# Attention times values of a head pair in two blocks, chunks ordered by size, the packed rows' tokens in one matmul

## The chip, the core and the metric

One core of a Trainium2 chip runs the whole program in one launch. The metric is the device time in microseconds; the median of the runs counts. The core has a matrix engine (PE, with its weight loads shown apart as PEld), a vector engine (DVE), a scalar engine (ACT), a general engine (POOL) and a queue engine (SP) that issues transfers. Each engine takes its instructions in the order in which they stand in its queue and waits on semaphores of the others.

## What is computed

The reference is causal attention with a cumulative bias, for 8 batches of 8 heads, 576 tokens and 64 dimensions, followed by a mixture of 8 experts with one expert for each of the 4608 tokens.

```python
scores = scale * np.matmul(q, k.transpose(0, 1, 3, 2))
s_pos = np.maximum(s, 0.0)
cum = np.cumsum(s_pos, axis=-1)
bias = -(cum[:, :, :, None] - cum[:, :, None, :])
scores = np.where(causal, -1000000000.0, scores + np.minimum(bias, 0.0))
scores = scores - np.max(scores, axis=-1, keepdims=True)
attn = np.exp(scores)
attn = attn / (np.sum(attn, axis=-1, keepdims=True) + 1e-09)
x = np.matmul(attn, v)          # then (batch, token, head * dim)
...
logits = x @ w_gate + modality_bias[modality_id]
e_idx = np.argmax(logits, axis=1)
for e in range(E):
    h = np.maximum(x[mask] @ w1[e], 0.0)
    out[mask] = gate_w[mask, None] * (h @ w2[e])
```

## The kernel before

The program has two stages. Attention fills a little less than the first half of the span, the experts (class `Moe`) the rest; the routing of tokens (class `Route`) runs in the background of both. The change touches attention alone.

**Pairs and chunks.** Attention works on 32 pairs. A pair is one head of two batches, called a and b. Its 2 x 576 query rows are cut into nine chunks: chunks 0 to 3 are 128 rows each of a, 4 to 7 the same of b, and chunk 8 holds the last 64 rows of a and the last 64 of b, packed into 128 partitions. Because of the causal mask, chunk c (or 4 + c) needs only 128(c + 1) keys, so chunks 3 and 7 are the largest (512 keys), 0 and 4 the smallest (128 keys, computed as 256), and chunk 8 needs 576.

**One chunk.** `score` issues two matmuls into an `sp` tile of PSUM (L228 and L229; four times two of 288 columns for chunk 8, L242 and L243). DVE adds the mask and takes the row extreme (L231, L245), ACT takes the exponential and the row sum into `sums` (L251). Three steps of the loop later (`LAG`) `trans` transposes the chunk, 128 x 128 at a time, on PE into a `pt` tile (L261; chunk 8 in L270, four into one tile and one into another). There are two `pt` buffers. ACT copies the transposed chunk to the SBUF tile `PT` (L264); for chunk 8 DVE does it (L276, four copies: a and b of the first tile, a and b of the second). So a transposition has to wait until the `pt` tile of the one before last has been copied out.

**The end of a pair.** `tail` multiplies the transposed weights by V: twelve matmuls with 64 output rows, a and b beside each other (L299 into `om` for queries 128 to 575, L297 into `ox` for queries 0 to 127). ACT and DVE copy the result to `oT` (L305, L306, L309), DVE adds a small number to the row sums and inverts them (`rs`, L303 and L304). Then two groups of small matmuls (`pw_`, L203) turn `oT` back to tokens and multiply it by the gate's weights in the same pass: two of 144 columns for each half, and in the second half two more of 72 columns for the packed tokens, one for a and one for b. DVE scales the result into `x` (L321, L323). Both halves use the same single `ox` buffer.

**The next pair's inputs.** `prep` splits the next pair's queries and keys into a high and a low part: POOL rounds them (L178: `QH`, `KA`, `KB`) and subtracts (L196, L198), and DVE makes one subtraction, the low part of a's queries (`QL`, L192). `QH` and `KA` have two buffers each, so POOL's first step for pair n + 1 waits until the last scores of pair n - 1 have read them.

**What sets the order.** `run` walks over pairs and over the nine chunks in the order of `ORDER`, and at each step issues a score, a step of `prep`, a step of the tail and a transposition. A scheduler then orders each engine's queue from this program order and its own estimates; `issue_after` ties the tail's matmuls behind those recorded before, and everything after them behind the last one (`wall`).

Of the kernel before, what the change touches and what calls it, by code (L numbers as in the profile page):

```python
# [7 lines left out]
F32 = mybir.dt.float32  # L8
# [4 lines left out]
ALU = mybir.AluOpType  # L13
# [18 lines left out]
class Attn:  # L32
# [71 lines left out]
    def setup(self, wg):  # L104
        nc = self.nc
        wgv = wg.rearrange("(h d) e -> d h e", d=64)
        for ab in range(2):
            nc.sync.dma_start(self.pw[64 * ab:64 * ab + 64, :, XW * ab + 64:XW * ab + XW], wgv)

    def consts(self, t1):  # L110
        nc = self.nc
# [23 lines left out]
        for ab in range(2):  # L135
            rows = slice(64 * ab, 64 * ab + 64)
# [3 lines left out]
        for ab in range(2):  # L140
            rows = slice(64 * ab, 64 * ab + 64)
            idv = self.ident[rows, 64 * ab:64 * ab + 64]
            nc.scalar.copy(self.pw[rows, :, XW * ab:XW * ab + 64], idv.unsqueeze(1).broadcast_to([64, 8, 64]))

    def rows0(self):
        nc = self.nc
        for u in range(2):
            nc.sync.dma_start(self.QL[u].bitcast(F32)[64:74], self.oh[:10])
            for ab in range(2):
                nc.sync.dma_start(self.KB[u].bitcast(F32)[74:76, ab], self.m1[:2])  # L150
# [124 lines left out]
                        w = PT[ab][:kp, PTW - 64:].unsqueeze(1)  # L275
                    cp(w, pt[:kp, :P * nj].rearrange("p (j a q) -> p a j q", a=2, q=64)[:, ab])  # L276

    def tail(self, st):

        nc = self.nc  # L280
        V, PT, x, h = st["V"], st["PT"], st["x"], st["h"]
        for _ in range(TD):
            yield
        o0 = self.ps2.tile([P, 512], F32, name="ox")
        om = self.ps2.tile([P, 448], F32, name="om")
        oT = self.oT[st["pi"] % 2]

        pe, self.pe = self.pe, []
        for j in (0, 1, 2, 3, 4, -1):
            q0 = max(P * j, P)  # L290
            for ab in range(2):
                r = slice(64 * ab, 64 * ab + 64)
                with ExitStack() as after:
                    for i in pe:
                        after.enter_context(self.tc.issue_after(i))
                    if j < 0:
                        m = nc.tensor.matmul(o0[r, :P], V[:, ab, 0, :], PT[ab][:, :P], start=True, stop=True)  # L297
                    else:
                        m = nc.tensor.matmul(om[r, q0 - P:], V[:, ab, j, :], PT[ab][:, PTS * j + q0 if j < 4 else PTW - 64:PTS * j + KW if j < 4 else PTW], start=j == 0, stop=j == 4)  # L299
                pe = [m.ins]  # L300
        self.wall = m.ins
        rs = self.sm.tile([P, 9], F32, name="rs")
        nc.vector.tensor_tensor(rs, st["sums"], self.eps, ALU.add)  # L303
        nc.vector.reciprocal(rs, rs)  # L304
        nc.scalar.copy(oT[:, :P], o0[:, :P])  # L305
        nc.scalar.copy(oT[:, P:512], om[:, :384])  # L306
        for ab in range(2):
            r = slice(64 * ab, 64 * ab + 64)
            nc.vector.tensor_copy(oT[r, 512 + 64 * ab:576 + 64 * ab], om[r, 384:])  # L309
        yield  # L310
        for g in range(2):
            xo = self.ps2.tile([P, 512], F32, name="ox")
            for u in range(2):
                c = 2 * g + u
                self.pw_(xo[:, 2 * XW * u:2 * XW * u + 2 * XW], oT[:, P * c:P * c + P], self.pw[:, h, :], start=True, stop=True)
            if g == 1:
                for ab in range(2):
                    self.pw_(xo[:, 4 * XW:5 * XW], oT[:, 512:], self.pw[:, h, XW * ab:XW * ab + XW], start=ab == 0, stop=ab == 1)
            src = xo[:, :4 * XW].rearrange("p (t d) -> p t d", t=4)
            rv = rs[:, 4 * g:4 * g + 4].unsqueeze(2).broadcast_to([P, 4, XW])  # L320
            nc.vector.tensor_tensor(x[g][:, :, :, h], src.rearrange("p t (d r) -> p t d r", r=2), rv.rearrange("p t (d r) -> p t d r", r=2), ALU.mult)  # L321
            if g == 1:
                nc.vector.tensor_scalar(x[2][:, 0, :, h], xo[:, 4 * XW:5 * XW].rearrange("p (d r) -> p d r", r=2), rs[:, 8:9], None, ALU.mult)  # L323
            yield

    def run(self, npair, newx, done, setup):

        bg = []
        self.load(1)
        seq = [(pi, i) for pi in range(npair) for i in ORDER]  # L330
        sts = {}
        prev, prepg, n = None, None, len(seq)
        for k in range(n + LAG + 9):
            if k < n:
                pi, i = seq[k]
                if k % 9 == 0:
                    sts[pi] = self.start(pi, newx(pi // 8) if pi % 8 == 0 else sts[pi - 1]["x"])
                    prepg = self.prep(pi + 1) if pi + 1 < npair else None
# [8 lines left out]
                    self.load(pi + 2)  # L347
                if prepg is not None:
                    next(prepg, 0)
            nt = None  # L350
            if LAG <= k < n + LAG:
                p0, i0 = seq[k - LAG]
                if i0 == ORDER[-1]:
                    nt = sts[p0]
            if prev is not None:
                if next(prev, 0) == 0:
                    prev = None
                    if ps["pi"] % 8 == 7:
                        bg.append(done(ps["pi"] // 8, ps["x"]))
            if LAG <= k < n + LAG:  # L360
# [4 lines left out]
            if prev is None and k >= n + LAG:  # L365
                break
            if bg and next(bg[0], 0) == 0:
                bg.pop(0)
        assert prev is None
        return bg  # L370


# [628 lines left out]
```

## Time and profile before

| | us |
|---|---|
| median of 3 runs | 925.4 |
| lowest and highest run | 919.98 and 928.19 |
| the profiled execution: its own time | 927.42 |
| its span | 925.7 |
| first matmul of the experts begins | 452.2 |

The profiled execution is one run; its time is 2.0 us above the median. In the timeline rows the columns are start, length, engine, line, operation, output tile <- inputs, shape, count, and in brackets the idle time of the engine before the row and what ended it. A count behind an x merges equal neighbours. Matmuls overlap, so on PE the distance from one start to the next says what a matmul costs, not its length.

### The profile page before, as it was taken

The numbers are of one execution on the slowest core, as the hardware profiler recorded it, in microseconds if no ns is written. First come the engines' busy times: TensorE is split into PE (matmuls) and PEld (weight loads), VectorE is DVE, ScalarE is ACT, GpSimd is POOL, SyncE is SP. The second block draws the span as 40 slices with busy tenths as digits, with TensorE's granted clock in tenths as the row PEclk, the third lists the DMA queues.
The fourth block names the chain that finished last, engine by engine and source line by source line (L and its number), as shares of the span: only waits on it lengthen the run. The fifth ranks groups of instructions, "written<-read, shape, count | busy, mean of one in ns | idle before, by whom it ended". The sixth has DMA issues, their size and how long they took to land. (4 is left out here: it accounts for less than half of the span.)

```text
span 925.7 us, 16704 instructions
## 1 busy us (share of the span) xinstructions
PE 836.3 (90%) x5584; PEld 697.8 (75%) x5584; DVE 622.3 (67%) x1486; ACT 521.4 (56%) x1209; POOL 573.5 (62%) x478
## 2 busy tenths in 40 slices
PE   0799998899889998799879989999999999999994
PEld 0577777677767776567669889999999999999962
DVE  7477777577867788666656966656666656666681
ACT  3577776677667776577434434545544445444651
POOL 9677777877697777853175536555655556555770
PEclk9999999999999999899989999999999999999998
DMA  5654445544544445520849758666666666665940
GB/s 148 197 136 137 137 136 150 176 134 133 173 149 151 125 133 179 229 83 3 277 164 332 282 203 301 236 221 228 230 225 219 224 223 224 223 228 220 336 160 2
DMA packets 67562, 172.76 MB, mean 187 GB/s; under 512 B 12087, under 2 KB 12087, under 8 KB 67412
## 3 DMA queue, kind: packets, MB, share of 16 engines
q1 hardware_dynamic: 61620, 151.64, 48.5%
q0 software_dynamic: 5856, 20.06, 5.5%
q8 instruction: 44, 0.72, 0.3%
q14 instruction: 42, 0.34, 0.1%
HBM read 144.95 MB, written 26.80 MB: 186 GB/s over the span
## 5 line engine op out<-in xcount | busy, mean ns | idle before, releaser
L251 ACT ACTIVATE pe<-pe,mx 128x512 f32<-128x512 f32 (+3 forms) x256 | 144.1, 564 | 48.7 <-DVE mx L231 46.7
L261 PE MATMUL pt<-ident,pe 128*128 128x128 f32 x640 | 121.1, 290 | 24.7 <-ACT PT L264 17.0
L231 DVE CUSTOM_DVE_ANT_0 pe<-sp,mk 128x512 f32<-128x512 f32 (+3 forms) x256 | 117.2, 481 | 22.9 <-PE sp L229 14.7
L264 ACT COPY PT<-pt 128x512 f32<-128x512 f32 (+3 forms) x256 | 106.6, 419 | 45.2 <-PE pt L261 34.6
L815 ACT ACTIVATE hT<-hp 128x512 fp32r<-128x512 f32 x72 | 42.8, 595 | 157.4 <-PE hp L813 156.5
L799 POOL DMA_INDIRECT out<-ys,oi x36 | 36.9, 1025 | 136.3 <-DVE ys L798 50.5
L261 PEld LDWEIGHTS pt<-ident,pe 128*128 128x128 f32 x640 | 79.9, 147 | 54.7 <-ACT PT L264 34.1
L228 PE MATMUL sp<-KA,QH 128*128 128x256 f32 (+2 forms) x256 | 98.2, 390 | 20.1 <-DVE KA L196 16.0
L196 POOL TENSOR_TENSOR KA<-rawk,KA 64x576 fp32r<-64x576 f32 x63 | 97.4, 1566 | 4.8 <-issue 2.3
L299 PE MATMUL om<-PT,V 128*64 128x448 f32 (+3 forms) x640 | 93.5, 435 | 0.0
L229 PE MATMUL sp<-KB,QL 76*128 76x256 f32 (+2 forms) x256 | 84.7, 334 | 7.2 <-DMA QL<-oh 7.2
L813 PE MATMUL hp<-xT,wcb 128*128 128x256 f32 x648 | 90.2, 283 | 0.0
L178 POOL TENSOR_SCALAR QH<-rawq 128x576 fp32r<-128x576 f32 x62 | 41.7, 674 | 74.6 <-issue 62.3
L816 DVE SCALAR_TENSOR_TENSOR hT<-hp,hT 128x512 fp32r<-128x512 f32 x72 | 49.3, 685 | 56.7 <-ACT hT L815 56.7
L813 PEld LDWEIGHTS hp<-xT,wcb 128*128 128x128 f32 x648 | 83.7, 189 | 0.6
L813 PE MATMUL hp<-xT,wcc 128*128 128x256 f32 x528 | 76.9, 286 | 7.9 <-DVE hT L816 3.2
L299 PEld LDWEIGHTS om<-PT,V 128*64 128x64 f32 x640 | 45.1, 142 | 48.8 <-issue 39.3
L792 PE MATMUL y<-wcb,hT 128*128 128x512 f32 x336 | 81.1, 398 | 0.0
L813 PE MATMUL hp<-xT,wca 128*128 128x256 f32 x552 | 78.2, 284 | 0.4 <-ACT xT L778 0.3
L813 PEld LDWEIGHTS hp<-xT,wcc 128*128 128x128 f32 x528 | 70.2, 194 | 9.2 <-DVE hT L816 3.4
L792 PEld LDWEIGHTS y<-wcb,hT 128*128 128x128 f32 x336 | 62.8, 188 | 14.8
L813 PEld LDWEIGHTS hp<-xT,wca 128*128 128x128 f32 x552 | 71.8, 190 | 1.3 <-ACT xT L778 0.5
(269 smaller groups left out, 1948.8 us busy)
## 6 DMA issues: line engine op xcount, KB each, us to landing
wrbw<-in_w SPq DMA_DIRECT2D x104, 512.0 KB
wraw<-in_w SPq DMA_DIRECT2D x56, 512.0 KB
rawq<-in_qkv SPq DMA_DIRECT2D x32, 576.0 KB
rawk<-in_qkv SPq DMA_DIRECT2D x32, 576.0 KB
xg<-lists SPq DMA_DIRECT2D x18, 576.0 KB
V<-in_qkv SPq DMA_DIRECT2D x32, 320.0 KB
lists<-z SPq DMA_DIRECT2D x8, 576.0 KB
ekd<-ek SPq DMA_DIRECT2D x1, 1440.0 KB
```

Of the source, the lines that this page charges most:

```text
L196: i = (nc.vector if pi == 0 and a == 0 else nc.gpsimd).tensor_tensor(KA[up, a], rk[up, a], KAf[up, a], ALU.subtract)
L228: self.pe.append(nc.tensor.matmul(sp[:, :nn], QH[:, q0:q0 + P], KA[:, ab, :nn], start=True, stop=False).ins)
L229: self.pe.append(nc.tensor.matmul(sp[:, :nn], QL[:EXT, q0:q0 + P], KB[:EXT, ab, :nn], start=False, stop=True).ins)
L231: ins = nc.vector.tensor_tensor_reduce(out=t[:, :n], in0=sp[:, :n], in1=self.mk[:, 512 - n:512], scale=-0.125, scalar=3.0e38, op0=ALU.add, ...
L251: nc.scalar.activation(t[:, :n], t[:, :n], AF.Exp, bias=m, scale=-1.0, accum_out=st["sums"][:, o:o + 1])
L261: self.pe.append(nc.tensor.transpose(out=pt[:, P * j:P * j + P], in_=pe[:, P * j:P * j + P], identity=self.ident).ins)
L264: cp(w[:, :, v:v + P], pt[:, :P * (c + 1)].rearrange("p (j q) -> p j q", q=P))
L299: m = nc.tensor.matmul(om[r, q0 - P:], V[:, ab, j, :], PT[ab][:, PTS * j + q0 if j < 4 else PTW - 64:PTS * j + KW if j < 4 else PTW], star ...
L792: self.last[0] = nc.tensor.matmul(y[u], hT[:, a, f, P * u:P * u + P], W[4 + f // 2][:, c, 512 * (f % 2):512 * (f % 2) + 512], start=f == 0 ...
L813: nc.tensor.matmul(hp[:, u], W[k][:, a, f:f + P], xT[:, c, k], start=k == 0 and i == 0, stop=k == 3 and i == 2)
L815: nc.scalar.activation(hs, hp, AF.Relu)
L816: nc.vector.scalar_tensor_tensor(hT[:, 1, 2 * m:2 * m + 2], hp, 0.0, hs.bitcast(F32), ALU.max, ALU.subtract)
```

## The change

Four things are changed in attention, and one tile shares its memory with another to make room.

- `ORDER` goes from (3, 7, 2, 1, 8, 6, 5, 0, 4) to (3, 7, 2, 6, 8, 1, 5, 0, 4): chunk 6 changes places with chunk 1, so that all chunks of the last queries come first.
- `tail` becomes two shorter tails for each pair. The first (`g` = 1), started when chunk 8 has been transposed, takes queries 256 to 575 in ten matmuls; the second (`g` = 0), started when the last chunk has been transposed, takes queries 0 to 255 in four. Each has its own `rs`, `oT` copy and `x`. The PSUM tiles `om` and `ox` become `o` (320 columns) and `ox`, one buffer each.
- In the first of these blocks the packed tokens come from one matmul of 72 columns with a new constant `pq` in place of two.
- `rs` is tied behind the latest row extreme (`hold`), the other matmuls' ties are looser within a step.

```diff
-ORDER = (3, 7, 2, 1, 8, 6, 5, 0, 4)
+ORDER = (3, 7, 2, 6, 8, 1, 5, 0, 4)
...
+        self.pq = c.tile([P, 8, XW], F32, name="pq")
...
-            s8 = t1.tile([64, KW], F32, name="s8")
+            s8 = sr
...
+            nc.sync.dma_start(self.pq[64 * ab:64 * ab + 64, :, 64:], wgv)
...
+            nc.scalar.copy(self.pq[rows, :, :64], idv.unsqueeze(1).broadcast_to([64, 8, 64]))
...
-    def tail(self, st):
+    def tail(self, st, g):
...
-        o0 = self.ps2.tile([P, 512], F32, name="ox")
-        om = self.ps2.tile([P, 448], F32, name="om")
+        q0, q1 = (256, KW) if g else (0, 256)
+        o = self.ps2.tile([P, 320], F32, name="o")
...
-        for j in (0, 1, 2, 3, 4, -1):
-            q0 = max(P * j, P)
+        nj = 5 if g else 2
+        for j in range(nj):
+            f = max(P * j, q0)
...
-                    if j < 0:
-                        m = nc.tensor.matmul(o0[r, :P], V[:, ab, 0, :], PT[ab][:, :P], start=True, stop=True)
-                    else:
-                        m = nc.tensor.matmul(om[r, q0 - P:], V[:, ab, j, :], PT[ab][:, PTS * j + q0 if j < 4 else PTW - 64:PTS * j + KW if j < 4 else PTW], start=j == 0, stop=j == 4)
-                pe = [m.ins]
+                    m = nc.tensor.matmul(o[r, f - q0:q1 - q0], V[:, ab, j, :], PT[ab][:, PTS * j + f if j < 4 else PTW - 64:PTS * j + q1 if j < 4 else PTW], start=j == 0, stop=j == nj - 1)
+            pe = [m.ins]
...
+        rs = self.sm.tile([P, 5], F32, name="rs")
+        with self.tc.issue_after(self.hold[0]):
+            nc.vector.tensor_tensor(rs[:, :n], st["sums"][:, 4 * g:4 * g + n], self.eps[:, :n], ALU.add)
+            nc.vector.reciprocal(rs[:, :n], rs[:, :n])
...
-            if g == 1:
-                for ab in range(2):
-                    self.pw_(xo[:, 4 * XW:5 * XW], oT[:, 512:], self.pw[:, h, XW * ab:XW * ab + XW], start=ab == 0, stop=ab == 1)
+        if g:
+            self.pw_(xo[:, 4 * XW:5 * XW], oT[:, 512:], self.pq[:, h, :], start=True, stop=True)
...
-            if nt is not None:
-                prev, ps = self.tail(nt), nt
+                if i0 in (8, ORDER[-1]):
+                    g = int(i0 == 8)
+                    prev.append((self.tail(sts[p0], g), sts[p0], g))
```

The lines below are instructions in the order in which they stand on an engine, in the middle of attention. Lines of the new program are three higher than those of the old around `score` and `trans` (L231 there is L228 before, L232 is L229, L264 is L261, L273 is L270, L279 is L276, L195 is L192, L267 is L264).

PE before, from the last two scores of a pair (256 columns, chunks 0 and 4) over the transposition of chunk 8 (`pep`) to the next pair's first scores (512 columns, chunks 3 and 7):

```order
L228 MATMUL sp<-KA_102,QH_98 128x256
L229 MATMUL sp<-KB_104,QL_100 128x256
L270 MATMUL pt<-ident,pep 128x128 x4
L228 MATMUL sp<-KA_102,QH_98 128x256
L270 MATMUL pt<-ident,pep 64x128
L229 MATMUL sp<-KB_104,QL_100 128x256
L228 MATMUL sp<-KA_103,QH_99 128x512
L229 MATMUL sp<-KB_105,QL_101 128x512
L228 MATMUL sp<-KA_103,QH_99 128x512
L229 MATMUL sp<-KB_105,QL_101 128x512
L261 MATMUL pt<-ident,pe 128x128 x5
```

The same place on PE now, from chunk 4's scores:

```order
L231 MATMUL sp<-KA_103,QH_99 128x256
L232 MATMUL sp<-KB_105,QL_101 128x256
L273 MATMUL pt<-ident,pep 128x128 x4
L273 MATMUL pt<-ident,pep 64x128
L231 MATMUL sp<-KA_102,QH_98 128x512
L232 MATMUL sp<-KB_104,QL_100 128x512
L264 MATMUL pt<-ident,pe 128x128 x2
L300 MATMUL o<-PT_108,V 64x320
L300 MATMUL o<-PT_106,V 64x320
```

Between chunk 8's transposition and the next one there is now one large score in place of two, and right behind that next transposition (chunk 1, two tiles) stands the first block of products with V.

DVE before, the stretch in which chunk 8's transposed tiles are copied out (L276), with the row extremes of the smallest chunks (`ISA`, 128 columns) around it:

```order
L321 TENSOR_TENSOR x<-ox,rs 128x144x2
L323 TENSOR_SCALAR xq<-ox,rs 128x36x2
L231 ISA pe,mx<-sp,mk 128x128
L231 ISA mx 128x1
L276 COPY PT_107<-pt 128x4x64
L276 COPY PT_108<-pt 128x4x64
L276 COPY PT_107<-pt 64x64
L276 COPY PT_108<-pt 64x64
L231 ISA pe,mx<-sp,mk 128x128
```

DVE now, the same stretch:

```order
L234 ISA pe,mx<-sp,mk 128x128
L234 ISA mx 128x1
L234 ISA pe,mx<-sp,mk 128x128
L234 ISA mx 128x1
L195 TENSOR_TENSOR QL_100<-rawq,QH_98 64x576
L279 COPY PT_108<-pt 128x4x64
L279 COPY PT_106<-pt 128x4x64
L279 COPY PT_108<-pt 64x64
L279 COPY PT_106<-pt 64x64
L234 ISA pe,mx<-sp,mk 128x512
```

The subtraction `QL` for the next pair now stands directly ahead of the copies in 24 of its 31 places; before, it stood behind the row extremes of the next pair's chunks 3, 7 and 2, and in none of them directly ahead of the copies.

ACT before, from the next pair's first exponential (512 columns) to the copy of chunk 3 (four tiles):

```order
L251 ACTIVATE pe,sums<-pe,mx 128x512
L264 COPY PT_108<-pt 128x2x128
L251 ACTIVATE pe,sums<-pe,mx 128x512
L264 COPY PT_107<-pt 128x128
L251 ACTIVATE pe,sums<-pe,mx 128x384
L264 COPY PT_108<-pt 128x128
L251 ACTIVATE pe,sums<-pe,mx 128x256
L264 COPY PT_106<-pt 128x4x128
```

ACT now:

```order
L254 ACTIVATE pe,sums<-pe,mx 128x512
L303 COPY oT_109<-o 128x256
L267 COPY PT_107<-pt 128x2x128
L267 COPY PT_106<-pt 128x128
L254 ACTIVATE pe,sums<-pe,mx 128x512
L267 COPY PT_107<-pt 128x128
L267 COPY PT_108<-pt 128x4x128
L254 ACTIVATE pe,sums<-pe,mx 128x384 x2
```

The copies of the small chunks no longer alternate one by one with exponentials of 512, 384 and 256 columns.

More of the change, by code (lines that the diff above doesn't have):

```diff
@@ new lines, in tail @@
+        rs = self.sm.tile([P, 5], F32, name="rs")
+        with self.tc.issue_after(self.hold[0]):
+            nc.vector.tensor_tensor(rs[:, :n], st["sums"][:, 4 * g:4 * g + n], self.eps[:, :n], ALU.add)
+            nc.vector.reciprocal(rs[:, :n], rs[:, :n])
+        xo = self.ps2.tile([P, 512], F32, name="ox")
+        for u in range(2):
+            c = 2 * g + u
+            self.pw_(xo[:, 2 * XW * u:2 * XW * u + 2 * XW], oT[:, P * c:P * c + P], self.pw[:, h, :], start=True, stop=True)
+        if g:
+            self.pw_(xo[:, 4 * XW:5 * XW], oT[:, 512:], self.pq[:, h, :], start=True, stop=True)
@@ L349, in run @@
                     next(prepg, 0)
-            nt = None
+            if prev and next(prev[0][0], 0) == 0:
+                _, st, g = prev.pop(0)
+                if g == 0 and st["pi"] % 8 == 7:
+                    bg.append(done(st["pi"] // 8, st["x"]))
             if LAG <= k < n + LAG:
                 p0, i0 = seq[k - LAG]
[L353 to L360, printed above, removed]
                 with self.behind():
                     self.trans(sts[p0], i0)
-            if nt is not None:
-                prev, ps = self.tail(nt), nt
-            if prev is None and k >= n + LAG:
+                if i0 in (8, ORDER[-1]):
+                    g = int(i0 == 8)
+                    prev.append((self.tail(sts[p0], g), sts[p0], g))
+            if not prev and k >= n + LAG:
                 break
@@ L368, in run @@
                 bg.pop(0)
-        assert prev is None
+        assert not prev
         return bg
```

32 lines of the change are left out of this document (12 added, 20 removed).

## The prediction

> **What bounds the kernel now.** I read first the busy time by windows, to see whether attention can be treated as one repeated pair. The columns are the window, its length, then busy time and count of PE, PEld, DVE, ACT and POOL, the granted clock, and the transfer engines' share and rate.
>
> ```profile
> 200.00:250.00 50.00, 46.15 (x337) 35.82 (x336) 38.39 (x142) 34.54 (x112) 34.67 (x37) 0.97 0.44 137
> 500.00:900.00 400.00, 394.27 (x2497) 353.73 (x2496) 268.41 (x293) 195.70 (x241) 233.73 (x105) 0.99 0.65 238
> ```
>
> In attention PE is busy 92% of the window and every other engine 77% or less. The experts keep PE busy 98%; the change doesn't touch their work, so what attention gains or loses reaches the end one to one.
>
> Next, the timeline of PE over one pair.
>
> ```profile
> 203.97 0.27 PE L261 MATMUL pt<-ident,pe 128*128 128x128 f32 x1
> 204.71 0.65 PE L261 MATMUL pt<-ident,pe 128*128 128x128 f32 x4 [0.46 <-ACT PT L264]
> 205.29 2.70 PE L299 MATMUL om<-PT,V 128*64 128x448 f32 x20
> ...
> 208.14 0.66 PE L261 MATMUL pt<-ident,pe 128*128 128x128 f32 x4
> ...
> 208.82 0.34 PE L229 MATMUL sp<-KB,QL 76*128 76x384 f32 x1
> 209.00 0.65 PE L203 MATMUL ox<-pw,oT 128*128 128x144 f32 x4
> 209.49 0.49 PE L261 MATMUL pt<-ident,pe 128*128 128x128 f32 x3
> ...
> 210.21 1.16 PE L203 MATMUL ox<-pw,oT 128*128 128x144 f32 x8
> 211.20 0.27 PE L261 MATMUL pt<-ident,pe 128*128 128x128 f32 x1
> 211.22 0.36 PE L228 MATMUL sp<-KA,QH 128*128 128x256 f32 x1
> 211.43 0.28 PE L229 MATMUL sp<-KB,QL 76*128 76x256 f32 x1
> 211.55 0.71 PE L270 MATMUL pt<-ident,pep 128*128 128x128 f32 x5
> 212.01 0.37 PE L228 MATMUL sp<-KA,QH 128*128 128x256 f32 x1
> ...
> 212.34 0.39 PE L228 MATMUL sp<-KA,QH 128*128 128x512 f32 x1
> ...
> 212.81 0.40 PE L228 MATMUL sp<-KA,QH 128*128 128x512 f32 x1
> ...
> 214.01 0.34 PE L229 MATMUL sp<-KB,QL 76*128 76x384 f32 x1
> 214.34 0.33 PE L261 MATMUL pt<-ident,pe 128*128 128x128 f32 x1
> ...
> 216.57 0.66 PE L261 MATMUL pt<-ident,pe 128*128 128x128 f32 x4 [0.46 <-ACT PT L264]
> ```
>
> From 204.71 to 216.57 a pair takes 11.86 us. PE is a nearly closed queue: five transpositions take 0.46 (211.55 to 212.01), about 0.1 each. What isn't work is a few waits. Between 203.97 and 204.71 one transposition takes 0.74, so about **0.63** is waiting: the four transpositions of chunk 3 need a `pt` tile that ACT hasn't emptied. From 214.01 to 214.34 the second half of a 384-column score takes 0.33 instead of 0.18 (208.82 to 209.00): **0.15**, again for `pt`. So the two `pt` buffers, and whoever empties them, are the weak place.
>
> **The change, part by part.** All terms are per pair.
>
> *The waits that go.* In ACT's new order chunk 0's copy precedes the 512-column exponential instead of following it, and chunks 4's and 3's stand together. A copy then waits for its transposition only, and 0.63 + 0.15 = 0.78 can go. If ACT still comes late, nothing goes. I take **-0.78**, bounds -0.78 and 0.
>
> *The packed tokens.* The group of four at 209.00 takes 0.49; the group of eight at 210.21, which has the two products of 72 columns besides, takes 0.99. The two cost at most 0.50, of which about 0.1 is the second group's wait for the single `ox`. One goes: **-0.20**, bounds -0.25 and -0.10. The wait for `ox` goes too, since other work now lies between the halves: **-0.10**, bounds -0.10 and 0.
>
> *The products with V in two blocks.* The columns summed over the matmuls of one half are 448 + 448 + 320 + 192 + 64 + 128 = 1600 before and 3 x 320 + 192 + 64 + 256 + 128 = 1600 now, so the streaming time stays. But a second block has its own borders. These are the weight loads at both borders of today's block:
>
> ```profile
> 205.29 0.20 PEld L299 LDWEIGHTS om<-PT,V 128*64 128x64 f32 x4 [0.17 <-issue]
> ...
> 208.14 0.42 PEld L261 LDWEIGHTS pt<-ident,pe 128*128 128x128 f32 x4 [0.17 <-PE om L299]
> ```
>
> The load starts only with its matmul, after 0.17 of idling, at each border: **+0.30** for two more borders, bounds +0.17 (one of the two hidden) and +0.40 (each with a little of the first matmul's start besides).
>
> *The new wait.* This is the term that decides. In the new PE order, chunk 8's transposition fills both `pt` tiles; one large score later stands chunk 1's transposition, which needs the first tile back, and the products with V are tied behind it. On DVE the copies that empty this tile now stand behind `QL`, which needs POOL's `QH`, which needs the last score of a to be done. Rows for this chain, first of the timeline, then of two views that group an operation's instructions (the first with shortest, median and longest in ns, the second with busy time and mean):
>
> ```profile
> 211.74 0.67 POOL L178 TENSOR_SCALAR QH<-rawq 128x576 fp32r<-128x576 f32 x1 [3.26 <-issue]
> 212.38 0.67 POOL L178 TENSOR_SCALAR KA<-rawk 128x576 fp32r<-128x576 f32 x1
> ...
> 203.17 1.17 DVE L192 TENSOR_TENSOR QL<-rawq,QH 64x576 fp32r<-64x576 f32 x1
> ...
> 204.40 0.25 ACT L264 COPY PT<-pt 128x128 f32<-128x128 f32 x1
> ...
> L192 DVE TENSOR_TENSOR QL<-rawq,QH x32: 741/1168/1495, 13.7 to 419.7; 64x576 fp32r<-64x576 f32 x32
> ...
> L276 DVE COPY PT<-pt 128x256 f32<-128x256 f32 x60 | 22.7, 419 | 5.8 <-PE sp L229 3.4 <-PE pt L270 1.7 <-PE sp L228 0.7
> ```
>
> I count from the start of chunk 0's score. PE's own work up to chunk 1's transposition is chunk 0, chunk 8's transposition, chunk 4 and one large score: the same four pieces that take 211.22 to 212.81 today, 1.59. The other path: POOL's `QH` starts 0.52 after (211.74), and POOL's next step begins at 212.38, so `QH` is done at 1.16, visible to DVE about 0.1 later (an estimate: ACT's copy ends at 204.65, PE goes on at 204.71). `QL` takes 1.17, two copies 0.42 each, 0.06 to PE: 1.16 + 0.10 + 1.17 + 0.84 + 0.06 = 3.33. PE waits 3.33 - 1.59 = **+1.74**. With the shortest `QL` in the row (0.74) it is +1.31; with the longest (1.50) +2.07.
>
> Which length of `QL` is right depends on POOL. The row at 203.17 ends at 204.34, and POOL's rounding before it ends at 203.74:
>
> ```profile
> 202.43 1.31 POOL L178 TENSOR_SCALAR KB<-rawk 64x576 fp32r<-64x576 f32 x2
> 203.82 3.18 POOL L196 TENSOR_TENSOR KA<-rawk,KA 64x576 fp32r<-64x576 f32 x2
> ```
>
> So `QL` ran 0.60 after POOL's instruction had ended, and seems to have stood still before. In the new place POOL goes from `QH` of a straight to its next 0.67 step before DVE hears of it; `QL` then stands about 0.57 and runs 0.60: 1.17 again, the value taken. The Trainium skill says the same in "SBUF — State Buffer", section "SBUF: two separate sides": the port pair that DVE and POOL share is an exclusive lock, held for a whole instruction, for a DVE operation with two SBUF inputs against a POOL operation that reads SBUF. By that rule the wait on PE is the +1.74, without it the +1.31; the trace agrees with the rule at 203.74.
>
> In 24 of 31 places `QL` stands directly ahead of the copies. In the other pairs the chain is chunk 8's transposition, two copies and chunk 1: the copies' 0.84 and about 0.2 for the matmul's end and hand-overs, less the large score of 0.47 (212.34 to 212.81): **+0.6**, bounds 0 and +0.9.
>
> *DVE's second `rs`.* One more addition and inversion of a few columns. The additions that stand today:
>
> ```profile
> L303 DVE TENSOR_TENSOR rs<-sums,eps x32: 155/652/3548, 39.4 to 442.9; 128x9 f32<-128x9 f32 x32
> ```
>
> The new one comes while POOL waits for the last score (the 3.26 of idling at 211.74), so I take 0.16 to 0.2, on DVE alone, and nothing on the path: its cover is that `QL` waits for POOL anyway. Without that cover it costs 0.5 more in each of the 24 pairs.
>
> *Routing.* Three times the counting matmuls of the router stand in PE's queue and wait for DVE:
>
> ```profile
> PE ox L501 <- DVE ohb L495: 7.4, 3, 2.5
> ```
>
> They move from inside the block of products to a place ahead of chunk 8's scores, with DVE busier. I take +1 each, **+3** in all, bounds -3 and +7.5 (the waits halve, or double). `pq` costs two transfers and two copies in the first pairs, hidden behind the 40 us before the first block; at worst 1 us. The transfers issued by SP in `prep` and `load` keep their loop steps, a pair ahead of use.
>
> **The sum.** For 24 pairs: -0.78 - 0.20 - 0.10 + 0.30 + 1.74 = +0.96, together +23.0. For the other 8: -0.78 - 0.20 - 0.10 + 0.30 + 0.6 = -0.18, together -1.4. Routing +3. In all **+24.6 us** on the profiled execution, 927.4 to 952. That execution lies 2.0 above the median of 925.4, so the median should be **950**.
>
> **Rivals.** About 1% (9 us) is what a measurement of this kernel can tell from no change.
>
> *Faster: the copies are not held.* If chunk 1's transposition finds its tile empty, the wait is 0 and each pair gains 0.78 + 0.20 + 0.10 - 0.30 = 0.78, 25 us in 32 pairs, 900. The point from which it decides is a new wait of 0.78. For it speaks that DVE idles a quarter of the window; against it, that DVE takes its queue in order, and even the shortest `QL` gives 1.31. Chance 0.07.
>
> *No change: a wait of about 0.8.* `QL` would need 0.74 and its start would have to come 0.5 earlier, with POOL not held by the last score; the 3.26 of idling at 211.74 speaks against it. 925. Chance 0.06.
>
> *Slower still: `rs` on the path.* If the first block's `rs` is held by a POOL instruction as today's is (0.65 in the middle of attention, 3.55 at most), it delays the row extremes of the small chunks and so `QL`: 0.5 in 24 pairs, 12 us more, 962. For it speaks the median of 652 in the row, against it POOL's idle time there. Chance 0.15.
>
> That the work is not what the change says is excluded by the order: ten and four products, one packed matmul.
>
> **Range and chances.** The forecast has 0.72. Its low end takes `QL` at 0.74 (-0.43 x 24 = -10) and routing at -3 instead of +3: 934. Its high end keeps half of ACT's waits (+0.39 x 32 = +12) and takes routing at +7.5 (+4.5): 966, which holds the third rival. With 2 us of spread below, that is 932 to 966, which leaves out the faster and the unchanged case, 0.13, and the tails. Slower by over 1%: 0.72 + 0.15 = 0.87; faster 0.07; the same 0.06.
>
> **What would show it.** Right: a PE row of two transpositions (chunk 1) with over 1.2 us of idling ahead, ended by DVE's `PT` copy, in 24 pairs; a pair of about 12.8 us; `QL` near 1.2 us and directly ahead of the copies in time; no 0.46 us of idling ahead of chunk 3's transpositions; two records of twelve fewer per pair in the small products of L203. Wrong: that idling missing or below 0.8, `QL` at 0.75, ACT rather than DVE ending PE's waits, or a pair below 11.9 us.

## The result and the profile after

| | before | after |
|---|---|---|
| time, median (lowest to highest), 4 runs each | 923.81 us (919.98 to 928.19) | 947.25 us (945.66 to 952.48) |
| ratio, with its 95% interval | | 1.0256 (1.023 to 1.0281): slower |
| the profiled execution: time, span | 927.42, 925.7 us | 945.66, 943.9 us |
| granted clock over the span | 0.974 | 0.977 |
| a plain pair, from the start of chunk 3's score to the next | 11.86 us | 12.62 us |
| start of the experts' first matmul (`hp`) in the span | 452.2 us | 469.0 us |
| from there to the end | 473.5 us | 474.9 us |

The profiles of e9 and e10 are of executions that ran slower than the others of the same kernel (1604.52 us and 971.14 us), so of these two kernels only the times are used.

The loss lies in attention: 16.8 of the 18.2 us between the two profiled executions have gone by when the experts begin. The same two windows as before, columns as there:

```profile
200.00:250.00 50.00, 44.84 (x348) 36.12 (x348) 35.58 (x139) 35.78 (x112) 33.68 (x36) 1.00 0.40 126
500.00:900.00 400.00, 393.63 (x2531) 357.09 (x2532) 260.40 (x292) 191.15 (x237) 224.69 (x103) 0.99 0.66 241
```

PE is busy 90% of the attention window instead of 92%. Over exactly one plain pair (200.48 to 212.34 before, 210.51 to 223.12 now), with a granted clock of 1.00 in both, its busy time falls from 11.40 to 11.18 us and its idle time grows from 0.46 to 1.43. The kernel isn't slower because PE has more to do; it waits more. The timeline of PE over the pair from the transpositions of chunk 3 and the short block of products to the second half of the small products (start, duration, and in brackets the idling ahead and what ended it):

```profile
204.92 0.60 PE L264 MATMUL pt<-ident,pe 128*128 128x128 f32 x4
...
206.53 0.87 PE L300 MATMUL o<-PT,V 128*64 128x256 f32 x8
207.34 0.65 PE L264 MATMUL pt<-ident,pe 128*128 128x128 f32 x4
...
208.07 0.66 PE L206 MATMUL ox<-pw,oT 128*128 128x144 f32 x4
208.56 0.49 PE L264 MATMUL pt<-ident,pe 128*128 128x128 f32 x3
...
209.42 0.36 PE L231 MATMUL sp<-KA,QH 128*128 128x256 f32 x1
...
210.82 0.40 PE L232 MATMUL sp<-KB,QL 76*128 76x512 f32 x1
212.66 0.41 PE L264 MATMUL pt<-ident,pe 128*128 128x128 f32 x2 [1.43 <-DVE PT L279]
212.99 2.27 PE L300 MATMUL o<-PT,V 128*64 128x320 f32 x20
215.20 0.44 PE L264 MATMUL pt<-ident,pe 128*128 128x128 f32 x2
...
215.94 0.65 PE L206 MATMUL ox<-pw,oT 128*128 128x144 f32 x4
216.43 0.34 PE L206 MATMUL ox<-pq,oT 128*128 128x72 f32 x2
216.61 0.27 PE L264 MATMUL pt<-ident,pe 128*128 128x128 f32 x1
```

Chunk 1's two transpositions at 212.66 stand still for 1.43 us, and DVE's copy of `PT` ends it. A score of 512 columns goes from its first half to the next instruction in 0.55 (the row at 215.39 to 215.94 in the same timeline), so the one that began at 210.51 would have let PE go on at 211.06. Counted from start to start the wait is therefore 1.60. DVE and POOL in the same stretch:

```profile
208.62 0.16 DVE L312 TENSOR_TENSOR rs<-sums,eps 128x4 f32<-128x4 f32 x1
...
209.94 1.30 POOL L181 TENSOR_SCALAR QH<-rawq 128x576 fp32r<-128x576 f32 x2 [3.92 <-issue]
...
210.64 1.20 DVE L195 TENSOR_TENSOR QL<-rawq,QH 64x576 fp32r<-64x576 f32 x1
...
211.77 1.00 DVE L279 COPY PT<-pt 128x256 f32<-128x256 f32 x4
...
216.85 0.31 DVE L312 TENSOR_TENSOR rs<-sums,eps 128x5 f32<-128x5 f32 x1
```

This is the predicted chain in time: `QH` starts 0.52 after chunk 0's score (209.42), `QL` takes 1.20 and ends at 211.84, the copies stand directly behind it, and PE goes on 3.24 us after that score. The waits of all engines over attention (in total, how often, the longest) show the same in sum, and a second thing. The first two rows are of the kernel before, from 50 to 452 us, the others of the changed kernel, from 50 to 469:

```profile
PE pt L261 <- ACT PT L264: 16.8, 31, 2.1
...
PE pt L261 <- DVE PT L276: 1.0, 2, 0.6
...
PE pt L264 <- DVE PT L279: 50.8, 31, 8.5
...
DVE QL L195 <- POOL QH L181: 15.5, 6, 6.7
...
PE pt L273 <- ACT PT L267: 3.9, 2, 3.8
```

PE's waits for ACT's copies are down from 16.8 us to 3.9 in two places. Those for DVE's copies grow from 1.0 to 50.8. In the timeline 19 of the 31 last 1.42 to 1.44 each; two last over 8 us. These two are where the router works in the background. The first of them:

```profile
168.43 0.96 POOL L523 DMA_INDIRECT lists<-xq,di  x1 [0.30 <-issue]
169.43 1.31 POOL L181 TENSOR_SCALAR QH<-rawq 128x576 fp32r<-128x576 f32 x2
170.14 1.21 DVE L195 TENSOR_TENSOR QL<-rawq,QH 64x576 fp32r<-64x576 f32 x1 [6.75 <-POOL QH L181]
...
172.16 0.66 PE L264 MATMUL pt<-ident,pe 128*128 128x128 f32 x2 [8.45 <-DVE PT L279]
```

POOL issues the router's transfers ahead of `QH`. `QL` stands idle 6.75 us for it on DVE, the copies behind `QL` wait with it, and PE waits 8.45. The three pairs there take 49.10 us instead of 44.02, the three of the second such place 47.82 instead of 43.84.

### The profile page after: what moved, and what is told of

It is laid out like the page before. It is cut to its first block, busy times and chain, and to the rows that moved or that the text cites. A ratio compares the mean times of both kernels' runs of the same rounds, so it can differ in the third digit from the quotient of the medians.

```text
span 943.9 us, 16901 instructions
## 1 busy us (share of the span) xinstructions
PE 823.7 (87%) x5648; PEld 697.1 (74%) x5648; DVE 634.6 (67%) x1550; ACT 522.4 (55%) x1211; POOL 577.0 (61%) x478
## 5 line engine op out<-in xcount | busy, mean ns | idle before, releaser
L264 PE MATMUL pt<-ident,pe 128*128 128x128 f32 x640 | 120.5, 287 | 51.1 <-DVE PT L279 50.8
L267 ACT COPY PT<-pt 128x512 f32<-128x512 f32 (+3 forms) x256 | 105.4, 422 | 87.8 <-PE pt L264 84.2
L234 DVE CUSTOM_DVE_ANT_0 pe<-sp,mk 128x512 f32<-128x512 f32 (+3 forms) x256 | 120.8, 485 | 30.3 <-PE sp L232 26.9
L264 PEld LDWEIGHTS pt<-ident,pe 128*128 128x128 f32 x640 | 76.2, 146 | 71.8 <-issue 60.9
L796 POOL DMA_INDIRECT out<-ys,oi x36 | 39.9, 1110 | 136.0 <-DMA out<-ys,oi 52.8
L231 PE MATMUL sp<-KA,QH 128*128 128x256 f32 (+2 forms) x256 | 100.7, 401 | 19.4 <-DVE KA L199 16.0
L300 PE MATMUL o<-PT,V 128*64 128x320 f32 (+4 forms) x896 | 105.6, 376 | 0.0
L300 PEld LDWEIGHTS o<-PT,V 128*64 128x64 f32 x896 | 60.7, 141 | 43.9 <-issue 15.4
L199 POOL TENSOR_TENSOR KA<-rawk,KA 64x576 fp32r<-64x576 f32 x63 | 89.6, 1441 | 4.6 <-DMA lists<-x,di 2.1
L232 PE MATMUL sp<-KB,QL 76*128 76x256 f32 (+2 forms) x256 | 83.3, 333 | 7.1 <-DMA QL<-oh 7.1
L813 DVE SCALAR_TENSOR_TENSOR hT<-hp,hT 128x512 fp32r<-128x512 f32 x72 | 49.2, 684 | 55.7 <-ACT hT L812 55.7
```

The source lines that it names most:

```text
L199: i = (nc.vector if pi == 0 and a == 0 else nc.gpsimd).tensor_tensor(KA[up, a], rk[up, a], KAf[up, a], ALU.subtract)
L231: self.pe.append(nc.tensor.matmul(sp[:, :nn], QH[:, q0:q0 + P], KA[:, ab, :nn], start=True, stop=False).ins)
L232: self.pe.append(nc.tensor.matmul(sp[:, :nn], QL[:EXT, q0:q0 + P], KB[:EXT, ab, :nn], start=False, stop=True).ins)
L234: ins = nc.vector.tensor_tensor_reduce(out=t[:, :n], in0=sp[:, :n], in1=self.mk[:, 512 - n:512], scale=-0.125, scalar=3.0e38, op0=ALU.add, ...
L264: self.pe.append(nc.tensor.transpose(out=pt[:, P * j:P * j + P], in_=pe[:, P * j:P * j + P], identity=self.ident).ins)
L267: cp(w[:, :, v:v + P], pt[:, :P * (c + 1)].rearrange("p (j q) -> p j q", q=P))
```

## The experiments

Every kernel ran beside the kernel before on the same chip. The median of the kernel before was 923.7 us beside e1 to e4, 923.8 beside e5 to e8, 931.2 beside e9 to e11 and 930.5 beside e12, so between these groups only ratios are compared. A pair is always a plain one, far from the router. Some of these kernels add a line or two, so line numbers differ by as much.

### e1: QL behind the copies

`QL` stays on DVE, but is tied behind the copies of chunk 8.

```diff
+                with self.tc.issue_after(self.t8) if self.t8 is not None else ExitStack():
                     nc.vector.tensor_tensor(QL[lo, a, :KW], rq[lo, a], QHf[lo, a, :KW], ALU.subtract)
...
-                    cp(w, pt[:kp, :P * nj].rearrange("p (j a q) -> p a j q", a=2, q=64)[:, ab])
+                    self.t8 = cp(w, pt[:kp, :P * nj].rearrange("p (j a q) -> p a j q", a=2, q=64)[:, ab]).ins
```

> The changed kernel with one thing different: on DVE the subtraction QL stands behind the four copies of chunk 8's transposed tiles instead of ahead of them; PE, ACT and POOL keep their order but for a few places around the router. Theory (PE waits at chunk 1's transposition because these copies are late): PE's wait there falls from 1.6 us to about 0.5, a plain pair from 12.62 to about 11.55 us, and the 8.5 us waits of the router's pairs go; in all 25 to 32 us less than the changed kernel, about 917 us, ratio to the kernel before 0.985 to 1.00. Rival 1 (two blocks of products cost their borders and more DVE steps): nothing of the loss depends on QL, 943 us or more, pair above 12.4. Rival 2 (QL is only moved, and delays the next pair's row extremes by as much): about half of the gain, 932 us.

Measured: 946.07 us, ratio 1.0211 (1.0143 to 1.0278), pair 12.47. The expectation missed: most of the wait went, the time did not. The timeline of one pair (PE, POOL, DVE, ACT in order of time):

```profile
209.17 0.41 PE L266 MATMUL pt<-ident,pe 128*128 128x128 f32 x2 [0.36 <-DVE PT L281]
...
211.95 2.80 POOL L201 TENSOR_TENSOR KA<-rawk,KA 64x576 fp32r<-64x576 f32 x2
...
213.37 1.40 DVE L314 TENSOR_TENSOR rs<-sums,eps 128x5 f32<-128x5 f32 x1
...
217.54 0.35 ACT L305 COPY oT<-o 128x256 f32<-128x256 f32 x1
217.94 0.76 PE L208 MATMUL ox<-pw,oT 128*128 128x144 f32 x4 [0.58 <-ACT oT L305]
```

Chunk 1's wait is 0.36 instead of 1.43. With it gone the long block of products ends earlier, its `rs` comes earlier on DVE, and now falls into the second of POOL's two subtractions (each 1.40): the addition of 5 columns, 0.31 in the changed kernel, takes 1.40. What stands behind it on DVE comes late, and PE now waits for `oT`. That it is `rs` was a guess here; e5 and e6 test it.

### e2: QL later still

```diff
+                with self.tc.issue_after(self.hold[0]) if self.hold[0] is not None else ExitStack():
                     nc.vector.tensor_tensor(QL[lo, a, :KW], rq[lo, a], QHf[lo, a, :KW], ALU.subtract)
```

> The changed kernel with QL tied behind the row extreme of the next pair's chunk 2 or 6, so far behind chunk 8's copies; the scheduler then puts the next pair's first row extreme (512 columns, 0.61 us) directly ahead of the copies, and the first large score ahead of chunk 8's transposition on PE. Theory (the copies' lateness after that transposition is what costs, whoever causes it): chunk 1's transposition follows chunk 8's directly, nothing on PE covers the copies, the wait stays near 1.4 to 1.7 us, pair about 12.6, 940 to 948 us. Rival (QL itself, held by POOL, is the cause): the wait goes with QL, pair 11.6, about 918 us.

Measured: 933.21 us, ratio 1.0105 (1.0068 to 1.0142), pair 12.20; between the two expectations. The tie moved more than `QL`:

```profile
199.77 0.74 DVE L196 TENSOR_TENSOR QL<-rawq,QH 64x576 fp32r<-64x576 f32 x1
...
204.40 1.04 PE L274 MATMUL pt<-ident,pep 128*128 128x128 f32 x5
...
204.71 0.69 DVE L235 CUSTOM_DVE_ANT_0 pe<-sp,mk 128x512 f32<-128x512 f32 x1 [0.17 <-PE sp L233]
...
205.13 0.11 PEld L274 LDWEIGHTS pt<-ident,pep 128*64 128x64 f32 x1 [0.38 <-ACT PT L268]
...
205.32 1.00 DVE L280 COPY PT<-pt 128x256 f32<-128x256 f32 x4
...
206.22 0.41 PE L265 MATMUL pt<-ident,pe 128*128 128x128 f32 x2 [0.78 <-DVE PT L280]
```

A row extreme of 512 columns now stands ahead of the copies where `QL` stood, and chunk 1's transposition idles 0.78 instead of 1.43. Counted from start to start the difference is smaller: PE takes 1.82 from chunk 8's first transposition (204.40) to chunk 1's (206.22), and these five transpositions take 0.52 in the changed kernel (209.99 to 210.51), so 1.30 is waiting instead of 1.60. A part of it lies ahead of chunk 8's fifth transposition, whose weights wait for a copy of ACT. The pair is 0.42 shorter, of which this wait makes 0.30. So it isn't `QL` as such: whatever DVE must do between PE's transposition of chunk 8 and the copies lies on the path. `QL` itself takes 0.74 here, where POOL's step ends 0.1 after it begins.

### e3: the order alone

The new `ORDER`; one block of products, `rs` and packed tokens as before.

```diff
-ORDER = (3, 7, 2, 1, 8, 6, 5, 0, 4)
+ORDER = (3, 7, 2, 6, 8, 1, 5, 0, 4)
```

> The kernel before with the new chunk order alone; one block of products with V, two packed matmuls. QL stands directly ahead of chunk 8's copies here too, in 20 pairs. Theory: chunk 8's copies are late again, but what waits for them on PE is not the products with V directly and more scores lie between; a pair 0.2 to 0.4 above 11.86, routing pairs longer by some us, 930 to 940 us. Rival (the loss comes from the split): equal to the kernel before, ratio 0.995 to 1.005.

Measured: 936.7 us, ratio 1.014 (1.0112 to 1.0168), pair 12.33. The time is as expected, the pair a little longer (0.47 above the kernel before, expected were 0.2 to 0.4). `QL` with its 1.20 stands ahead of the copies here too; PE waits 0.58 for them.

### e4: the split alone

The two blocks, the second `rs` and the packed matmul with the old order; the long block comes after chunk 6.

```diff
-ORDER = (3, 7, 2, 6, 8, 1, 5, 0, 4)
+ORDER = (3, 7, 2, 1, 8, 6, 5, 0, 4)
...
-                if i0 in (8, ORDER[-1]):
-                    g = int(i0 == 8)
+                if i0 in (6, ORDER[-1]):
+                    g = int(i0 == 6)
```

> The changed kernel with the old chunk order; the block for the last queries starts when chunk 6 has been transposed. QL stands directly ahead of chunk 8's copies in 3 pairs alone. Theory: without the late copies the split costs its two more borders (0.2 to 0.3) and saves the packed matmul and the wait for ox (0.3) and part of ACT's waits: a pair of 11.4 to 12.1 us, 915 to 938 us. Rival (two blocks are what costs): a pair of 12.4 or more, 943 us or more.

Measured: 955.59 us, ratio 1.0358 (1.0306 to 1.041), pair 12.46. The theory as it was written there missed; the time and the pair lie where the rival put them. DVE and PE in the timeline:

```profile
215.69 1.20 DVE L195 TENSOR_TENSOR QL<-rawq,QH 64x576 fp32r<-64x576 f32 x1
...
216.82 0.44 DVE L322 TENSOR_TENSOR x<-ox,rs 128x288 f32<-128x288 f32 x1
217.18 1.00 DVE L279 COPY PT<-pt 128x256 f32<-128x256 f32 x4
...
218.07 0.74 PE L264 MATMUL pt<-ident,pe 128*128 128x128 f32 x5 [0.64 <-DVE PT L279]
```

The split by itself puts `QL` and, behind it, the product of the small matmuls with `rs` (L322) ahead of the copies. So each half of the change brings about the same neighbourhood on DVE. The plain pair is 0.60 longer than before; most of the loss lies elsewhere. The four pairs around each of the router's first two places take 67.2 and 65.0 us, counted from chunk 8's score, instead of 55.9 and 55.7 in the kernel before: 20.6 of the 28.2 us by which the experts start later (480.5 instead of 452.2). The losses aren't additive: 1.4% for the order and 3.6% for the split with its packed matmul, and 2.56% for all of it.

### e5 and e6: rs without its addition, with and without e1's tie

In both, `rs` is the reciprocal of the sums; the addition of 1e-9 is left out. The reciprocal has one SBUF input, the addition two.

```diff
-            nc.vector.tensor_tensor(rs[:, :n], st["sums"][:, 4 * g:4 * g + n], self.eps[:, :n], ALU.add)
-            nc.vector.reciprocal(rs[:, :n], rs[:, :n])
+            nc.vector.reciprocal(rs[:, :n], st["sums"][:, 4 * g:4 * g + n])
```

e5 has e1's tie besides:

> The kernel of e1 (QL behind chunk 8's copies) and rs without its addition: the reciprocal is taken of the row sums themselves, so the addition of 1e-9 (a DVE operation on two SBUF tiles) is left out. Theory (in e1 the wait moved to the second block's rs, which stood 1.40 us behind POOL's subtraction KA; the next row extremes, exponentials and the oT copy of the first block were late by it): PE's 0.58 us wait for ACT's oT goes, only the 0.36 ahead of chunk 1's transposition stays, a plain pair falls from 12.47 to 11.5 to 11.8, the whole to 915 to 928 us, no slower than the kernel before by more than 0.5%. Rival (the two blocks' own work on PE, their borders, is what remains): pair 12.2 or more, 938 us or more.

Measured: 914.29 us, ratio 0.9897 (0.9873 to 0.9922), pair 11.37; a little better than expected, and about 1% faster than the kernel before. e6 has `QL` where the change puts it:

> The changed kernel with rs without its addition and nothing else changed (1e-9 left out as in e5). Theory: in the changed kernel rs takes 0.16 to 0.31 and chunk 1's wait for QL decides; a pair stays at 12.3 to 12.65, 938 to 947 us. Rival (rs is the cause by itself): 12.0 or less, below 930 us.

Measured: 942.64 us, ratio 1.0206 (1.0179 to 1.0232), pair 12.62, as expected. e5 and e6 differ by the place of `QL` alone, and that is worth 28 us and 1.25 in each plain pair. Each edit alone takes the ratio from 1.0256 to 1.0211 and to 1.0206, half a per cent that the intervals don't separate from nothing; the two together gain 3.6%. So there are two waits, one behind the other: `QL` ahead of the copies hides that `rs` would be held by POOL, and the gain of the first edit shows only when the second is made.

### e7 and e8: the same edits in the kernel before

e7 leaves the addition out of `rs` in the kernel before:

```diff
-        nc.vector.tensor_tensor(rs, st["sums"], self.eps, ALU.add)
-        nc.vector.reciprocal(rs, rs)
+        nc.vector.reciprocal(rs, st["sums"])
```

> Control: the kernel before with rs without its addition (1e-9 left out). There rs takes 0.65 us and stands between the two row extremes of chunk 8, ahead of ACT's largest exponential, which the products with V cover. Theory: DVE is not late there, a pair stays at 11.7 to 11.86, 918 to 924 us. Rival (any DVE time is worth its length): 0.65 in 32 pairs, 903 us.

Measured: 923.63 us, ratio 1.0004 (0.9988 to 1.002), pair 11.86. In the kernel before `rs` costs nothing, though its addition took 0.65 there; its cover held.

e8 makes the packed matmul alone, with the constant `pq` and its room as in the change:

```diff
...
-                for ab in range(2):
-                    self.pw_(xo[:, 4 * XW:5 * XW], oT[:, 512:], self.pw[:, h, XW * ab:XW * ab + XW], start=ab == 0, stop=ab == 1)
+                self.pw_(xo[:, 4 * XW:5 * XW], oT[:, 512:], self.pq[:, h, :], start=True, stop=True)
```

> The kernel before with the packed tokens in one matmul and nothing else. Theory: PE is the closed queue, a matmul less is worth its 0.20 to 0.25 us in each of 32 pairs, 6 to 8 us, 916 to 918 us, ratio 0.990 to 0.994. Rival (the time is taken back by the next wait for a pt tile): ratio 0.997 to 1.002.

Measured: 916.04 us, ratio 0.9909 (0.988 to 0.9937), pair 11.64. Of the change's three parts this one is a gain, 0.22 per pair.

### e9 and e12: a third pt tile

The changed kernel with three `pt` tiles, and three `sp` tiles instead of four to make room. It tests the other half of the wait: that PE needs a tile, not the data in it.

```diff
-SPB = 4
+SPB = 3
...
-            pt = self.ps1.tile([P, 512], F32, name="pt")
+            pt = self.ps1.tile([P, 512], F32, name="pt", bufs=3)
...
-                pt = self.ps1.tile([P, 512], F32, name="pt")
+                pt = self.ps1.tile([P, 512], F32, name="pt", bufs=3)
```

> The changed kernel with three pt tiles instead of two, paid for with three sp tiles instead of four. Theory (chunk 1's transposition waits for the tile that chunk 8's copies empty, and these stand behind QL): that transposition then takes the third tile, which was emptied before, and its 1.4 us of idling goes. But the copies themselves come no earlier, and the block of products behind needs them: PE waits there instead, for 1.60 less chunk 1's own 0.41, about 0.8 to 1.2, ended by DVE's copy of PT. Pair 11.9 to 12.3, 925 to 938. Rival (the tile isn't what it waits for, or one score tile less costs as much): pair 12.6 or more, 943 or more.

Measured: ratio 1.0006 (0.9985 to 1.0027). The whole loss is gone, a little more than expected. Where PE waits is read from e12, which is the same kernel:

> The kernel of e9_third_pt once more, for a profile of it in which TensorE's matmuls have their usual durations (in e9's they last about twice as long, so no wait shows). Its time was that of the kernel before, 1.0006 times. Theory: the ratio is within 0.995 to 1.005 again, the pair is 11.8 to 12.0, and what is left of the wait (0.7 to 1.2 per pair) stands ahead of the five-chunk block of products, ended by DVE's copy of PT, not ahead of chunk 1's transposition. Rival (the tile only hid part of the wait, and the rest came from elsewhere): chunk 1's transposition still waits over 0.5, or the pair is below 11.4 with the time lost outside the plain pairs.

Measured: ratio 1.0001 (0.9975 to 1.0026), pair 12.15. One pair, DVE and PE:

```profile
205.51 1.20 DVE L195 TENSOR_TENSOR QL<-rawq,QH 64x576 fp32r<-64x576 f32 x1 [0.40 <-POOL QH L181]
...
206.65 1.00 DVE L279 COPY PT<-pt 128x256 f32<-128x256 f32 x4
...
207.11 2.60 PE L300 MATMUL o<-PT,V 128*64 128x320 f32 x20 [0.85 <-DVE PT L279]
```

`QL` and the copies stand as in the changed kernel. Chunk 1's transposition no longer waits. The block of products does, for the copies' data: 0.85 instead of 1.43, and ended by the same operation. The pair is longer than the 11.8 to 12.0 expected, and 0.29 longer than before. The time is nevertheless that of the kernel before. From the first pair's score of chunk 3 to the last pair's this profile is 7.6 us longer than that of the kernel before (420.4 instead of 412.8); the last pair's way from there to the first `hp` gives back 5.0 (18.4 us, 436.4 to 454.8, instead of 23.4, 428.8 to 452.2). The other 2.6 can't be placed, since that profile of the kernel before was taken on another occasion, at 927.42, and the kernel before ran at 930.5 beside e12.

### e10: the copies on ACT

```diff
-PTDVE = (8,)
+PTDVE = ()
```

> The changed kernel with chunk 8's two copies on ACT instead of DVE; QL stays where it is. Theory (QL on DVE's queue holds the copies): the wait ahead of chunk 1's transposition falls from 1.4 to below 0.6 and is ended by ACT; pair 11.5 to 12.0, 912 to 928, with ACT 0.8 busier per pair. Rival (the copies would be late on any engine, behind ACT's exponentials): the wait stays over 1.0, pair 12.3 or more, 937 or more.

Measured: ratio 1.0098 (1.0064 to 1.0133), between the two expectations. Taking the copies off DVE's queue recovers 1.6 of the 2.56%. What holds up the rest is not shown.

### e11: e5 with a third pt tile

The edits of e5 and of e9 together.

> The kernel of e5_ql_and_rs (QL behind the copies; rs as the reciprocal of the sums alone, the addition of 1e-9 left out) with three pt tiles and three sp tiles. Theory (with QL behind, chunk 1 waits 0.24 for the copies and little else is left of pt): at most 0.24 in 24 pairs to gain, 6 us: 908 to 914. Rival (one score tile less holds up the scores behind the exponentials): 0.2 or more per pair lost, 920 or more.

Measured: 908.28 us (907.61 to 908.48), ratio 0.9755 (0.9734 to 0.9777), pair 10.93. In us it lies in the expected range, but that range was written for a kernel before of 923.8, and this chip's is 931.2: by the ratio it is better than expected, and the best version found. The pair is 0.44 shorter than e5's, not 0.24. The same place in e5,

```profile
207.44 0.40 PE L233 MATMUL sp<-KA,QH 128*128 128x512 f32 x1
...
208.31 0.41 PE L266 MATMUL pt<-ident,pe 128*128 128x128 f32 x2 [0.24 <-DVE PT L281]
208.65 2.27 PE L302 MATMUL o<-PT,V 128*64 128x320 f32 x20
```

and in e11:

```profile
214.75 0.39 PE L266 MATMUL pt<-ident,pe 128*128 128x128 f32 x2
214.89 0.48 PE L233 MATMUL sp<-KA,QH 128*128 128x512 f32 x1
...
215.54 2.28 PE L302 MATMUL o<-PT,V 128*64 128x320 f32 x20
```

The score and the two transpositions go from 207.44 to 208.65, 1.21, in e5, and from 214.75 to 215.54, 0.79, in e11. By this comparison the wait that the profile showed as 0.24 of idling cost 0.42 from start to start. e11 also leaves the addition of 1e-9 out, as e5 does; the reference has it.

## Why the prediction was right, point by point

The forecast was 950 (932 to 966), slower; the result is 947.25. On the profiled executions the sum was +24.6, and +18.2 was measured. That execution of the kernel before lay 3.6 above the median of its four runs, that of the changed kernel 1.6 below its own, so the medians differ by 23.4. That the median came out within 3 us of the forecast is therefore luck in part; the profiled sum was off by 6.4. By its steps:

- **ACT's waits go (-0.78).** Right in the place: where 0.46 of idling stood ahead of chunk 3's transpositions there is none (204.92), and of `pt` waits on ACT 3.9 us are left in all. The 0.78 itself was not measured singly.
- **Packed tokens and `ox` (-0.20 - 0.10).** Right. The two halves of the small products took 0.49 + 0.99 before and take 0.49 (208.07 to 208.56) + 0.67 (215.94 to 216.61) now: -0.32. e8 has -0.22 for the packed matmul alone.
- **Two more borders (+0.30).** Too dear. One block took 2.85, the two take 0.81 (206.53 to 207.34) and 2.21 (212.99 to 215.20): +0.17, the lower bound.
- **The new wait (+1.74).** Right in place, cause and size: 1.60. Its chain was put at 3.33 from chunk 0's score and takes 3.24; PE's own work was put at 1.59 and takes 1.64. `QL` at 1.20 is the predicted 1.17, standing behind POOL's second `QH` for about half of it. One thing the prediction didn't see: at 210.64 `QL` starts behind the row extreme ahead of it on DVE (which ends at 210.58) as well as behind POOL's first `QH` (which ends at about 210.6), so the prediction's link to POOL alone is not shown for its start; its end, 0.60 after that of POOL's second `QH` (211.24), is as predicted. Idling above 1.2 us occurs in 22 pairs, 24 were predicted; in the other nine it is 0.2 to 1.1. That `QL` ahead of the copies is the cause is shown by e1 (tied behind them, 1.43 falls to 0.36) and by e5 against e6 (the tie takes 1.25 off the pair), and that the tile is what PE waits for by e12.
- **The sum of a plain pair.** -0.78 - 0.32 + 0.17 + 1.60 = +0.67, the first term as predicted and the others as measured; the pair grew by 0.76. The other 0.09 is not located. Predicted was +0.96.
- **Routing (+3, at most +7.5).** Mis-sized, and by another mechanism. The counting matmuls of the router, which waited 7.4 us in three places, wait no longer at all in attention. Instead `QL` waits up to 6.75 us for `QH` while POOL issues the router's transfers, and passes the wait on to PE through the copies. Two of the three router places lose 5.1 and 4.0 us; the third, with the pairs around it, is 1.3 shorter, and the pair behind that 1.2 longer: +9.0 in all, the new wait of these pairs included, and above the bound. The new wait and routing lean on the same link, which the prediction priced only where POOL is free to start `QH`.
- **The second `rs` (nothing).** Right for this kernel: e6, without the addition, has the same pair of 12.62. But the cover named was indeed a cover: once `QL` is moved, the same addition takes 1.40 and costs about as much as the wait that was removed (e1, 12.47, against e5, 11.37). The prediction put the price of a lost cover at 0.5; by these pairs it is 1.1.

The sum came out too high by 6.4 us, and it came this near because errors cancel. Counted between the scores of chunk 3, 13 pairs are plain ones and grow by 0.76, 9.8 together. The first four, in which `QL` doesn't stand ahead of the copies yet, grow by 0.1 together, and the three ahead of the router's places by 0.8 together. So the 20 pairs outside the router's places cost 10.7, where the prediction had +21.6 for all pairs without routing. The router's 11 pairs cost 9.0. The last pair's way to the experts, which the prediction didn't treat, is 2.9 shorter (23.4 to 20.5), and the experts end 1.4 later. The prediction's mechanism holds; its +0.96 in 24 pairs does not.

The rival "faster" asked for the copies not to be held; e5 shows that its mechanism was sound and its condition false. With the copies nearly free and `rs` shortened the pair is 11.37, 0.49 below before, and with a third tile 10.93, 0.93 below (the rival said 0.78).

On the exclusive lock that the Trainium skill describes ("SBUF — State Buffer", section "SBUF: two separate sides"), the runs agree at three places: `QL` takes 0.74 where POOL is about to fall idle (e2), 1.20 where POOL has just begun a step of 0.67 (the changed kernel), and the addition of 5 columns takes 0.16 to 1.40, the latter where it meets a subtraction of 1.40 at its beginning (e1). e5, which has only the reciprocal with its one input left, has none of e1's loss; that this reciprocal met POOL at the same moment is not shown.

What stays open: the last 0.1 of e2's pair and of the plain pair's sum, and how much of e10's rest is ACT's.

## What to carry to other kernels

When an order moves copies that empty a scarce buffer, look at what stands directly ahead of them on the copying engine and what that in turn waits for: here one subtraction, held in part by POOL, made PE wait 1.6 us in a plain pair and over 8 where POOL was busy with transfers. A removed wait may show nothing because a second one stands behind it, so test two suspects together as well as singly: half a per cent each alone was 3.6% jointly. And of a change in three parts, try each alone: the packed matmul was worth 0.9%. With a third `pt` tile, `QL` behind the copies and `rs` without its two-input addition the whole change, a loss as it stood, is part of a version that is 2.5% faster than the kernel before. That the order and the split are needed for this is not shown: the kernel before with the packed matmul and a third `pt` tile was not run.

## What the runs showed of the hardware unexpectedly

- In e1 an addition of 128 x 5 numbers took from 0.16 to 1.40 us. A long one (213.37 to 214.77) begins and ends with a subtraction of POOL (the second of the two from 211.95 to 214.75); that POOL holds it is read from this coincidence and from e5, where it is missing.
- POOL pays as well: two of its `KA` steps take 1.80 us at 211.21 in the changed kernel, beside the running part of `QL`, and 1.30 in e1 (208.80, the first row), where `QL` runs only after them:

```profile
208.80 1.30 POOL L182 TENSOR_SCALAR KA<-rawk 128x576 fp32r<-128x576 f32 x2
...
211.21 1.80 POOL L181 TENSOR_SCALAR KA<-rawk 128x576 fp32r<-128x576 f32 x2
```

- At two places a wait on PE cost more than the idling that its row shows: 0.24 shown, 0.42 from start to start (e11); 1.43 shown, 1.60 from start to start (the changed kernel).
